# Other places in the DMA queues for a fused gated-mix kernel's first rows, bias rows, gate rows and rows for sums

## Chip, cores and metric

One Trainium2 chip, one core. The time is the device time of one execution in microseconds (us), the median of several runs. Lower is better. The core has five engines that run their own instruction queues: TensorE (PE, with its weight loads shown apart as PEld), VectorE (DVE), ScalarE (ACT), GpSimd (POOL) and SyncE (SP). Transfers between main memory and the core's memory (DMAs) are issued from the queues of SP, ACT and POOL.

## What is computed

```python
x: [2048, 512]; wqkv: [512, 1536]; w_phi: [32, 16, 16]; wo: [512, 512]
w1: [512, 1792]; w2: [1792, 512]; b1, b2, gate_w                      # all float32

g   = sigmoid((x * gate_w).sum(-1, keepdims=True))
# A: linear attention, 32 heads of 16
q, k, v = heads(x @ wqkv)
pq, pk  = q @ w_phi, k @ w_phi                       # per head
phi     = lambda p: concat(softmax(p), softmax(-p))  # 32 features per head
kv, z   = phi(pk).T @ v, phi(pk).sum(over rows)
a       = concat_heads(phi(pq) @ kv / (phi(pq) @ z + 1e-6)) @ wo
# B: dense layer with squared ReLU
b       = relu(x @ w1 + b1) ** 2 @ w2 + b2
out     = g * a + (1 - g) * b
```

## The kernel before

Every float32 matrix product is made of three matmuls in a faster float format: each operand is split into a high part (`hi`, a copy by ScalarE) and a low part (`lo`, a subtraction by VectorE), and `mm3` adds hi*hi, hi*lo and lo*hi. So each weight or x tile that is loaded costs one ScalarE and one VectorE instruction before TensorE can use it (`split`, L64 and L67).

The rows of x are cut into four blocks of 512 (`NB`), each of four chunks of 128 (`NC`). The spine is a list of 56 work units: two sweeps over the hidden layer (7 pieces of 128 hidden columns each), in each sweep the four blocks, in each block the 7 pieces. Unit t makes `up` for a later piece (`u`, then bias, ReLU and square on ScalarE) and `down` for its own (`d`). Everything else is hung into this spine by hand: `at(slot, f, ...)` puts a step at a slot, two slots to a unit, and `run(slot)` calls the steps as the spine is traced. The first sweep carries the key and value side of the attention: the fold of `w_phi` into the key weights, then eight pairs of row chunks (`pair_steps`), pair p at slot 14 + 4.5p. A pair multiplies its rows with the folded weights in seven block products; some of these use sums and differences of rows (`sums`, four additions on POOL) and of weights (`joint`). Three of the weight combinations don't fit in the core's memory: they are stored in main memory once (`wkeep`, L214) and reloaded for each pair into three slots (`again`, L624, issued from ACT's queue right behind the read of the product before). The second sweep carries the query side and the output.

The steps that matter here:

- `start` loads the first x tiles and the first weights, one behind the other on SP's queue (`fetch`, L513), while ten warm-up matmuls run; the weights of the first piece come in a quarter of their own (`first_w(0, 0, 1)`).
- `joint_start` loads the four pieces of `wv` (L176); `tiles_fold` makes the fold on TensorE (L184), and four transposes on VectorE (`turned`, L197) turn it.
- `rows_alike` loads `gate_w` (`gwb`) and `b2` (`b2b`), repeated over 128 partitions (L843). `b2b` is first read where a block's output rows are begun (L876).
- `gate_load` loads a chunk's rows for the gate (L264, L266), 256 KB each; `gate_chunk` multiplies and sums them on VectorE (L271); `gates` ends a block's gates.
- `x_load(b)` loads the four x tiles of a block (L87); block 2's go out on POOL's queue. `x_split` splits them.
- `sums_load(p)` loads the rows for a pair's sums (L596), `sums` adds them on POOL (L603 to L606) and splits them (`sh`, `sl`).
- At the end of a block in the first sweep its four chunks are stored to main memory from POOL's queue (`part`, L887).

Loads of x, of weights and of the rows for sums share four buffers (`in`), gate rows, output rows and some others share six (`row`). A load that has no free buffer waits in its queue, and what is queued behind it waits too.

The order on each queue is set by a scheduler when the kernel is built: it goes by the order in which the steps are traced and by when it thinks that buffers come free, so that a load whose buffer is free can be put ahead of an earlier one whose buffer isn't. `tc.issue_after(i)` pins instructions of the same engine behind `i` in the queue; it is an order, not a wait. `st[...]` holds the instructions that serve as such pins, among them `row` (the last of the first weight rows), `summed` (the last addition of a pair), `stored` (the last store on POOL's queue). `behind()` pins splits and gate work behind the latest split of a hidden piece.

```python
s = b * SL + 2.5 * c - 1 if b > 1 else 17.5 + c / 2 if b else 3.5 + 2 * c   # slot of chunk c's gate rows
at(s + (4.5 if b == 1 else 3), gate_chunk, b * NC + c)
s, late = ((4, 2), (19.5, 1), (22, 2.5), (36, 2))[b]                        # slot of x_load(b + 1)
at(s - 2 - (p > 0), sums_load, p)                                          # s: the pair's first slot
```

Of the kernel before, what the change touches and what calls it, by code (L numbers as in the profile page):

```python
# [8 lines left out]
F32 = mybir.dt.float32  # L9
# [7 lines left out]
P = 128  # L17
S, D, H, DH, F = 2048, 512, 32, 16, 1792
NK = D // P
# [16 lines left out]
def tile_gated_mix(ctx: ExitStack, tc: tile.TileContext, xT, xn, wqT, wkT, wphi, wv, wo, w1, b1, w2, b2, gw, out):  # L36
# [47 lines left out]

    def load(src, eng=nc.sync):
        t = stage.tile([P, 512], F32, tag="in", name="in")
        eng.dma_start(t, src)  # L87
        return t

    def row():  # L90
        return work.tile([P, D], F32, tag="row", name="row", bufs=6)
# [73 lines left out]
    def joint_start(loaded):  # L165
        wph, *t = loaded
        two = lambda a: a.rearrange("p (h c) -> p h c", h=2)
        st["W"], st["raw"] = {}, {}
        tmp = work.tile([P, 4 * D], F32, tag="phiT", name="tmp", bufs=1)
        st["tmp"] = tmp[:, :2 * D], tmp[:, 2 * D:]  # L170
        st["slots"] = [work.tile([P, 2 * D], F32R, tag=t, name=f"slot{t}", bufs=1) for t in ("o0", "o1", "ez")]
        for k in (0, 2, 1, 3):
            r = st["tmp"][k // 2] if k % 2 else work.tile([P, 2 * D], F32, tag="e", name=f"raw{k}", bufs=2)
            st["raw"][k] = r
            with tc.issue_after(st["row"].ins):
                nc.sync.dma_start(two(r)[:, :, 256:], two(wv[k * P:(k + 1) * P, :]))  # L176

    def tiles_fold(loaded):
        wph, *t = loaded
# [78 lines left out]


    def gate_load(n):  # L260
        st["xn", n] = row()
        if n // NC == 1:
            with tc.issue_after(st["summed"].ins):
                nc.gpsimd.dma_start(st["xn", n], xn[n])  # L264
        else:
            nc.sync.dma_start(st["xn", n], xn[n])  # L266

    def gate_chunk(n):
        t = st["xn", n]
# [229 lines left out]
    def start():  # L499
        fs, wide = range(FIRST), FIRST * P  # L500
        W = [ffn_tiles("w1", f) for f in fs]
        ps = [p.tile([P, SB], F32, tag="s", name="u") for p in (ps_e, ps_b, ps_f)]
        xs = st["x", 0] = []
        for f in fs:
            up_w[f] = [tuple(z[:, P * f:P * (f + 1)] for z in W[k]) for k in range(NK - 1)]
            up_w[f].append(tuple(z[:, wide:] for z in W[f]))
        raw = [(stage.tile([P, 512], F32, tag="in", name="in"), row()) for _ in range(NK)]
        last = act = None

        def fetch(dst, src):  # L510
            nonlocal last
            with tc.issue_after(last.ins) if last else nullcontext():
                last = nc.sync.dma_start(dst, src)  # L513

        def first_w(k, a, b):
            fetch(raw[k][1][:, a * P:b * P].rearrange("p (f c) -> p f c", f=b - a),
                  w1[a:b, :, k * P:(k + 1) * P].rearrange("f p c -> p f c"))

        def follow(i, eng, *a):
            with tc.issue_after(i.ins) if i else nullcontext():  # L520
                return eng(*a)

        ready = small.tile([P, 1], F32, tag="den", name="ready", bufs=2)
        act = nc.scalar.activation(ready, st["zeros"][:, :1], AF.Copy)
        for k in range(NK):
            if k == 0:
                first_w(k, 0, 1)
            fetch(raw[k][0], xT[0, :, k, :])
            first_w(k, 0 if k else 1, FIRST)
        dve = None  # L530
        for k in range(NK):
            u, t = raw[k]
            xh, xl = (xpool.tile([P, SB], F32R, tag=g, name=f"{g}0_{k}") for g in ("xh", "xl"))
            xs.append((xh, xl))
            if k == 0:
                w = [(t[:, a:b], *(z[:, a:b] for z in W[k])) for a, b in ((0, P), (P, wide))]
            elif k < NK - 1:
                w = [(t[:, :wide], *(z[:, :wide] for z in W[k]))]
            else:
                w = [(t[:, P * f:P * (f + 1)], *(z[:, wide:] for z in W[f])) for f in fs]  # L540
            if k < 2:
                dve = follow(dve, nc.vector.tensor_copy, xh, u)
            else:
                act = follow(act, nc.scalar.activation, xh, u, AF.Copy)
            for src, hi, lo in w:
                act = follow(act, nc.scalar.activation, hi, src, AF.Copy)
            lows = [(lo, src, hi.bitcast(F32), ALU.subtract) for src, hi, lo in w]
            lows.insert(k == 0, (xl, u, xh.bitcast(F32), ALU.subtract))
            for x in lows:
                dve = follow(dve, nc.vector.tensor_tensor, *x)  # L550
            terms = [(f, 0, xh) for f in fs] + [(f, 0, xl) for f in fs] + [(f, 1, xh) for f in fs]
            if k == 0:
                terms.insert(1, terms.pop(6))
            if k == NK - 1:
                terms.sort(key=lambda x: x[0])
            for n, (f, part_, x) in enumerate(terms):
                st["up"] = follow(st["up"], lambda: nc.tensor.matmul(
                    ps[f], up_w[f][k][part_], x, start=k == 0 and (part_, x) == (0, xh),
                    stop=k == NK - 1 and part_ == 1))
        fetch(b1c, b1)  # L560
        do_w1(FIRST)
        for f in fs:
            hid[f] = hidden(f, ps[f])
            if f == 0:
                st["act0"] = st["act"]
        for p in (ps_e, ps_b, ps_f):
            used(p)

    def x_load(b):
        if b == 2:  # L570
            with tc.issue_after(st["summed"].ins):
                st["xin", b] = [load(xT[b, :, k, :], nc.gpsimd) for k in range(NK)]
        else:
            st["xin", b] = [load(xT[b % NB, :, k, :]) for k in range(NK)]
        st["x", b] = []
# [15 lines left out]
    def sums_load(p):  # L591
        b, c = ROWS[p]
        rows = xT[b].rearrange("p k (h c r) -> p k h c r", h=2, c=2)[:, :, :, c, :]
        st["rows", p] = [stage.tile([P, 2, 2, P], F32, tag="in", name="in") for _ in range(2)]
        for i, t in enumerate(st["rows", p]):
            nc.sync.dma_start(t, rows[:, 2 * i:2 * i + 2])  # L596

    def sums(p):
        a, d = st["rows", p]
# [180 lines left out]
        at(14.5, joint_last, j)  # L780
    for b in range(NB):
        for c in range(NC):
            s = b * SL + 2.5 * c - 1 if b > 1 else 17.5 + c / 2 if b else 3.5 + 2 * c
            at(s, gate_load, b * NC + c)
            at(s + (4.5 if b == 1 else 3), gate_chunk, b * NC + c)
        if c == NC - 1:
            at(s + 4.5 if b == 1 else s + 3, gates, b)
        s, late = ((4, 2), (19.5, 1), (22, 2.5), (36, 2))[b]
        at(s, x_load, b + 1)
        for k in range(NK):  # L790
            at(s + late + k / 2, x_split, b + 1, k)
# [51 lines left out]
            nc.sync.dma_start(t, src.partition_broadcast(P))  # L843

    at(2, rows_alike, gwb, gw)
    at(9, rows_alike, b2b, b2)
    warm_up()
    start()
    with tc.issue_after(st["act0"].ins):
# [85 lines left out]
```

## Time and profile before

| | |
|---|---|
| median of 3 runs | 511.15 us (511.1 to 512.4) |
| profiled execution | 512.31 us, span 510.5 us from first to last instruction |
| TensorE busy | 502.9 us (99%) |
| VectorE busy | 407.1 us (80%) |
| ScalarE busy | 256.6 us (50%) |
| POOL busy | 91.4 us (18%) |
| granted TensorE clock | 1.00 |
| moved by DMA | 76.13 MB, 149 GB/s on average |

All times inside the trace are microseconds from the start of the span. A row of a timeline gives the start, the duration, the engine, the line of the kernel, the operation and `out<-in`; `x4` means four instructions taken together, and what stands in brackets is the time that the engine was idle before and what ended it. `SPq` and `ACTq` are the queues of these engines, and a DMA row shows the issue, not the transfer. In the chain, a DMA's time runs from issue to landing. TensorE's busy time counts overlapping matmuls once; consecutive full matmuls start 0.23 us apart in most of the span.

### The profile page before, as it was taken

The page shows a single profiled execution, that of the slowest core. Times are in us where ns is not written, and L with a number is a line of the kernel's source. Part 1 is how long each engine was busy: PE and PEld are TensorE (multiplying, and loading weights), DVE is VectorE, ACT ScalarE, POOL GpSimd, SP SyncE. Part 2 cuts the span into 40 slices and gives each one's busy share as a digit, 9 for nine tenths or more (in the row PEclk, how much of TensorE's full clock was granted, in tenths as well). Part 3 has the DMA queues.
Part 4 walks back from the last instruction along what each step waited for, and adds up shares of the span by engine and source line. Part 5 has one row for each costly group of instructions (what it writes and reads, how often), then busy time and mean ns, then how long its engine had stood idle before and what let it go on. Part 6 is the DMA issues. An engine that isn't in the chain of part 4 may idle for free.

```text
span 510.5 us, 9358 instructions
## 1 busy us (share of the span) xinstructions
PE 502.9 (99%) x3522; PEld 406.3 (80%) x3522; DVE 407.1 (80%) x675; ACT 256.6 (50%) x458; POOL 91.4 (18%) x105
## 2 busy tenths in 40 slices
PE   8999998999999999999999999999999999999997
PEld 5878776888888888888888878788787878788775
DVE  5559958798975979796987989897969797897724
ACT  4778753467344564463565654444455344333540
POOL 0000460203420033100012141211212120111200
PEclk9999999999999999999999999999999999999999
DMA  8768486756843559862276221325112221041112
GB/s 258 256 234 263 176 284 246 221 208 208 318 172 132 198 170 314 299 206 88 76 198 221 65 91 41 105 57 156 48 31 86 70 86 44 8 131 56 37 28 82
DMA packets 46757, 76.13 MB, mean 149 GB/s; under 512 B 6904, under 2 KB 24056, under 8 KB 46712
## 3 DMA queue, kind: packets, MB, share of 16 engines
q1 hardware_dynamic: 37304, 42.37, 27.2%
q10 hardware_dynamic: 6624, 23.73, 13.1%
q0 software_dynamic: 2784, 9.44, 5.2%
q8 instruction: 28, 0.46, 0.4%
q14 instruction: 17, 0.14, 0.1%
HBM read 57.68 MB, written 11.54 MB: 136 GB/s over the span
## 4 chain that ended last, share of the span: by engine, by line
PE 90%; DMA 5%; ACT 2%; DVE 1%; issue 1%; SPq 0%; DVEq 0%
PE u L77 9%; PE d L77 9%; PE d L78 9%; PE d L79 9%; PE u L78 9%; PE u L79 9%; PE pX L636 3%; PE q L77 3%; PE att L78 3%; PE att L77 3%; PE att L79 3%; PE q L79 3%; PE q L78 3%; PE pX L638 3%; PE pX L637 3%; DMA sloto<-wkeep 3%
## 5 line engine op out<-in xcount | busy, mean ns | idle before, releaser
L421 ACT ACTIVATE r<-u,b1c 128x512 f32<-128x512 f32 x56 | 38.5, 688 | 128.0 <-PE u L79 126.1
L77 PE MATMUL d<-w2h,hh 128*128 128x512 f32 x222 | 86.9, 392 | 0.0
L78 PE MATMUL d<-w2l,hh 128*128 128x512 f32 x222 | 86.5, 390 | 0.0
L79 PE MATMUL d<-w2h,hl 128*128 128x512 f32 x222 | 86.4, 389 | 0.0
L77 PE MATMUL u<-xh,w1h 128*128 128x512 f32 x212 | 83.8, 395 | 0.6 <-ACT w1h L64 0.6
L78 PE MATMUL u<-xl,w1h 128*128 128x512 f32 x212 | 82.6, 390 | 0.0
L79 PE MATMUL u<-xh,w1l 128*128 128x512 f32 x212 | 82.5, 389 | 0.0
L336 POOL TENSOR_TENSOR ez<-e,z 128x512 f32<-128x512 f32 x32 | 43.3, 1374 | 166.0 <-ACT e L308 166.0
L67 DVE TENSOR_TENSOR hl<-r,hh 128x512 fp32r<-128x512 f32 x56 | 38.6, 691 | 24.6 <-ACT hh L64 24.6
L77 PEld LDWEIGHTS u<-xh,w1h 128*128 128x128 f32 x212 | 39.8, 188 | 12.1 <-issue 2.9
L77 PEld LDWEIGHTS d<-w2h,hh 128*128 128x128 f32 x222 | 41.7, 188 | 9.2 <-issue 0.6
L78 PEld LDWEIGHTS d<-w2l,hh 128*128 128x128 f32 x222 | 41.7, 188 | 8.9 <-DVE w2l L67 0.4
L79 PEld LDWEIGHTS d<-w2h,hl 128*128 128x128 f32 x222 | 41.7, 188 | 8.7
L79 PEld LDWEIGHTS u<-xh,w1l 128*128 128x128 f32 x212 | 39.8, 188 | 8.4
L78 PEld LDWEIGHTS u<-xl,w1h 128*128 128x128 f32 x212 | 39.8, 188 | 7.9
L311 DVE TENSOR_REDUCE sm<-e 128x64 f32<-128x1024 f32 x27 | 32.8, 1214 | 10.5 <-ACT e L308 10.5
L308 ACT ACTIVATE e<-e 128x1024 f32<-128x1024 f32 x27 | 28.6, 1059 | 23.2 <-DVE e L306 23.1
L64 ACT ACTIVATE hh<-r 128x512 fp32r<-128x512 f32 x56 | 35.2, 628 | 1.0
L422 ACT ACTIVATE r<-r 128x512 f32<-128x512 f32 x56 | 34.9, 623 | 0.7
L675 ACT ACTIVATE tmp<-pX 128x512 f32<-128x512 f32 x24 | 14.4, 598 | 32.7 <-PE pX L638 30.9
L374 ACT ACTIVATE phiT<-tb 32x256 f32<-32x256 f32 x64 | 26.4, 412 | 5.0 <-DVE tb L359 3.9
L343 DVE TENSOR_REDUCE dz<-ez 128x64 f32<-128x1024 f32 x16 | 19.4, 1212 | 11.5 <-POOL ez L336 11.5
(179 smaller groups left out, 989.2 us busy)
## 6 DMA issues: line engine op xcount, KB each, us to landing
sloto<-wkeep ACTq DMA_DIRECT2D x30, 512.0 KB, 4.0
in<-in_xT SPq DMA_DIRECT2D x44, 256.0 KB, 3.9
slotez<-wkeep ACTq DMA_DIRECT2D x15, 512.0 KB, 4.1
phiT<-tb SPq DMA_DIRECT2D x192, 32.0 KB, 1.8
in<-in_w SPq DMA_DIRECT2D x23, 256.0 KB, 3.7
part<-row POOLq DMA_DIRECT2D x16, 256.0 KB, 5.3
row<-part SPq DMA_DIRECT2D x16, 256.0 KB, 2.8
out<-row SPq DMA_DIRECT2D x15, 256.0 KB, 2.2
```

The costliest lines, as they stand in the source:

```text
L64: i = nc.scalar.activation(hi, src, AF.Copy)
L67: st["lo"] = elo.tensor_tensor(lo, src, hi.bitcast(F32), ALU.subtract)
L77: nc.tensor.matmul(o, ah[:, sa], bh[:, sb], start=first, stop=False)
L78: nc.tensor.matmul(o, ah[:, sa], bl[:, sb], start=False, stop=False)
L79: return nc.tensor.matmul(o, al[:, sa], bh[:, sb], start=False, stop=last)
L308: nc.scalar.activation(ef, ef, AF.Exp)
L311: nc.vector.tensor_reduce(sm, e3, AX.X, ALU.add)
L336: nc.gpsimd.tensor_tensor(ez[:, hs, :], e3[:, hs, :], zbc[half], ALU.mult)
L343: nc.vector.tensor_reduce(dz, ez, AX.X, ALU.add)
L374: nc.scalar.activation(dst, src, AF.Copy)
L421: st["relu"] = nc.scalar.activation(r, ps, AF.Relu, bias=b1c[:, fc:fc + 1])
L422: nc.scalar.activation(r, r, AF.Square)
```

## The change

- In `start` the weights' first quarter is issued from ACT's queue, and the first x is the first load of SP's queue. The first activation is pinned behind that issue.
- The four `wv` loads lose their pin on `row`.
- `b2b` is loaded at slot 2 instead of 9.
- Block 0's gate rows: chunk 0 moves from slot 3.5 to 5.5, and its `gate_chunk` with it from 6.5 to 8.5; chunks 0 and 1 are pinned behind the last `wv` load, 2 and 3 behind the latest load made by `load` (`in`).
- Block 1's gate rows: chunks 0 and 1 stay at slots 17.5 and 18; 2 and 3 are loaded inside `x_load(2)`, behind the third and fourth x tile, all in one chain on POOL's queue.
- Gate rows of blocks 2 and 3 are pinned behind the latest rows for sums on SP's queue (`ahead`).
- Pair 4's rows for sums are loaded from POOL's queue, behind the latest store there.

```diff
--- before.py
+++ after.py
@@ -84,7 +84,7 @@
 
     def load(src, eng=nc.sync):
         t = stage.tile([P, 512], F32, tag="in", name="in")
-        eng.dma_start(t, src)
+        st["in"] = eng.dma_start(t, src)
         return t
 
     def row():
@@ -172,8 +172,7 @@
         for k in (0, 2, 1, 3):
             r = st["tmp"][k // 2] if k % 2 else work.tile([P, 2 * D], F32, tag="e", name=f"raw{k}", bufs=2)
             st["raw"][k] = r
-            with tc.issue_after(st["row"].ins):
-                nc.sync.dma_start(two(r)[:, :, 256:], two(wv[k * P:(k + 1) * P, :]))
+            st["wv"] = nc.sync.dma_start(two(r)[:, :, 256:], two(wv[k * P:(k + 1) * P, :]))
 
     def tiles_fold(loaded):
         wph, *t = loaded
@@ -258,12 +257,10 @@
 
 
     def gate_load(n):
+        eng, pin = ((nc.sync, "in" if n > 1 else "wv"), (nc.gpsimd, "summed"), (nc.sync, "ahead"), (nc.sync, "ahead"))[n // NC]
         st["xn", n] = row()
-        if n // NC == 1:
-            with tc.issue_after(st["summed"].ins):
-                nc.gpsimd.dma_start(st["xn", n], xn[n])
-        else:
-            nc.sync.dma_start(st["xn", n], xn[n])
+        with tc.issue_after(st[pin].ins):
+            st["xrow"] = eng.dma_start(st["xn", n], xn[n])
 
     def gate_chunk(n):
         t = st["xn", n]
@@ -513,20 +510,18 @@
                 last = nc.sync.dma_start(dst, src)
 
         def first_w(k, a, b):
-            fetch(raw[k][1][:, a * P:b * P].rearrange("p (f c) -> p f c", f=b - a),
-                  w1[a:b, :, k * P:(k + 1) * P].rearrange("f p c -> p f c"))
+            return (raw[k][1][:, a * P:b * P].rearrange("p (f c) -> p f c", f=b - a),
+                    w1[a:b, :, k * P:(k + 1) * P].rearrange("f p c -> p f c"))
 
         def follow(i, eng, *a):
             with tc.issue_after(i.ins) if i else nullcontext():
                 return eng(*a)
 
         ready = small.tile([P, 1], F32, tag="den", name="ready", bufs=2)
-        act = nc.scalar.activation(ready, st["zeros"][:, :1], AF.Copy)
+        act = follow(nc.scalar.dma_start(*first_w(0, 0, 1)), nc.scalar.activation, ready, st["zeros"][:, :1], AF.Copy)
         for k in range(NK):
-            if k == 0:
-                first_w(k, 0, 1)
             fetch(raw[k][0], xT[0, :, k, :])
-            first_w(k, 0 if k else 1, FIRST)
+            fetch(*first_w(k, 0 if k else 1, FIRST))
         dve = None
         for k in range(NK):
             u, t = raw[k]
@@ -568,8 +563,15 @@
 
     def x_load(b):
         if b == 2:
-            with tc.issue_after(st["summed"].ins):
-                st["xin", b] = [load(xT[b, :, k, :], nc.gpsimd) for k in range(NK)]
+            st["xin", b] = []
+            for k in range(NK):
+                with tc.issue_after(st["summed"].ins):
+                    t = stage.tile([P, 512], F32, tag="in", name="in")
+                    st["summed"] = nc.gpsimd.dma_start(t, xT[b, :, k, :])
+                    st["xin", b].append(t)
+                if k > 1:
+                    gate_load(NC + k)
+                    st["summed"] = st["xrow"]
         else:
             st["xin", b] = [load(xT[b % NB, :, k, :]) for k in range(NK)]
         st["x", b] = []
@@ -593,7 +595,11 @@
         rows = xT[b].rearrange("p k (h c r) -> p k h c r", h=2, c=2)[:, :, :, c, :]
         st["rows", p] = [stage.tile([P, 2, 2, P], F32, tag="in", name="in") for _ in range(2)]
         for i, t in enumerate(st["rows", p]):
-            nc.sync.dma_start(t, rows[:, 2 * i:2 * i + 2])
+            if p == 4:
+                with tc.issue_after(st["stored"].ins):
+                    st["stored"] = nc.gpsimd.dma_start(t, rows[:, 2 * i:2 * i + 2])
+            else:
+                st["ahead"] = nc.sync.dma_start(t, rows[:, 2 * i:2 * i + 2])
 
     def sums(p):
         a, d = st["rows", p]
@@ -780,8 +786,9 @@
         at(14.5, joint_last, j)
     for b in range(NB):
         for c in range(NC):
-            s = b * SL + 2.5 * c - 1 if b > 1 else 17.5 + c / 2 if b else 3.5 + 2 * c
-            at(s, gate_load, b * NC + c)
+            s = b * SL + 2.5 * c - 1 if b > 1 else 17.5 + c / 2 if b else max(5.5, 3.5 + 2 * c)
+            if b != 1 or c < 2:
+                at(s, gate_load, b * NC + c)
             at(s + (4.5 if b == 1 else 3), gate_chunk, b * NC + c)
         if c == NC - 1:
             at(s + 4.5 if b == 1 else s + 3, gates, b)
@@ -843,7 +850,7 @@
             nc.sync.dma_start(t, src.partition_broadcast(P))
 
     at(2, rows_alike, gwb, gw)
-    at(9, rows_alike, b2b, b2)
+    at(2, rows_alike, b2b, b2)
     warm_up()
     start()
     with tc.issue_after(st["act0"].ins):
```

## The prediction

> **What bounds the kernel now.** I read the page's head first, then who TensorE (PE) waits for, then the chain of work that ended last, and only then the timelines of the stretches that these name.
>
> ```profile
> span 510.5 us, 9358 instructions
> PE pX L636 <- DMA sloto<-wkeep: 1.9, 2, 1.7
> PE u L77 <- ACT w1h L64: 0.6, 1, 0.6
> PE u L557 <- DVE xh L521: 0.3, 1, 0.3
> ```
>
> The last three rows are PE's own waits (total, times, longest). PE waits for data 2.8 us in all, in three places, and the rest of the span is matmuls one behind the other, apart from the start-up and the last store. So no edit can win more than these waits and what it takes off the start. The chain puts them in time:
>
> ```profile
> 33.14 3.70 DMA in<-in_w
> ...
> 64.77 4.71 DMA sloto<-wkeep
> ...
> 70.59 8.41 DMA sloto<-wkeep
> 79.04 0.50 PE pX L636
> ```
>
> The 0.6 is a weight piece issued at 33.14, split by ScalarE (ACT) and needed by `u`. The 1.7 is the reload at 70.59: it takes 8.41 us where the one at 64.77 took 4.71, and PE stands until 79.04. The third is the first x tile.
>
> **The change, part by part.**
>
> **1. The start.** The first x goes ahead of the first weights' quarter on SP's queue, and the quarter goes out on ACT's.
>
> ```profile
> 0.74 0.39 SPq L513 DMA_DIRECT2D row<-in_w  x1
> 1.19 0.41 SPq L513 DMA_DIRECT2D in<-in_xT  x1
> 0.74 1.28 ACT L524 ACT_TABLE_LOAD   x1 [0.74 <-PEq L924]
> 2.71 0.31 ACT L521 ACTIVATE w1h<-row 128x128 fp32r<-128x128 f32 x1 [0.48 <-DMA row<-in_w]
> 5.33 0.43 DVE L521 CAST xh<-in 128x512 fp32r<-128x512 f32 x1 [4.20 <-DMA in<-in_xT]
> 1.19 4.45 PE L496 MATMUL warm<-zeros 128*128 128x512 bf16 x10 [1.19 <-DVE zeros L490]
> 5.91 0.77 PE L557 MATMUL u<-xh,w1h 128*128 128x512 f32 x1 [0.27 <-DVE xh L521]
> 6.47 0.60 PE L557 MATMUL u<-xh,w1l 128*128 128x512 f32 x1
> 6.90 0.63 PE L557 MATMUL u<-xh,w1h 128*128 128x512 f32 x2
> 7.36 0.85 PE L557 MATMUL u<-xl,w1h 128*128 128x512 f32 x3
> ```
>
> The x's issue moves from 1.19 to 0.74, so all that hangs on it moves up 0.45 us at most. ACT gets one issue ahead of its table load, about 0.4 us by SP's first row; the weights' split at 2.71 may come that much later and is still over 2 us ahead of the x at 5.33, which hides it. Ten warm-up matmuls take 4.45 us, 0.45 each; the third real one starts 0.43 behind the second, and from 6.90 on two take 0.46, so 0.23 each. The array is slow until about 6.7. If that is a matter of time, a start 0.45 sooner buys one more slow matmul and loses 0.20 of it: worth 0.25 us. If it is a matter of how many matmuls went before, the whole 0.45 stays. I take 0.25, since warm-ups and real matmuls were equally slow over 5 us; the ends are 0 (the tile lands no sooner) and 0.45.
>
> The Trainium skill's page "TensorE: Matmul & The Clock Gate", section "Part 1: The HAM clock gate (the "warmup" mystery)", says that the clock opens after a busy window of some 3.4 us that runs freely, a matter of time and not of the number of matmuls; it speaks against this part, and by it the start is worth 0.25, by a count 0.45. The slow spacing up to 6.7, 5.5 us behind the first warm-up, agrees with a gate, though the granted clock of this profile reads full speed throughout, and one switch in one run can't tell time from count.
>
> **2. Bias rows at slot 2, wv without its pin, first gate rows later.**
>
> ```profile
> 28.62 0.59 SPq L843 DMA_DIRECT2D b2b<-in_b  x1
> 29.25 1.70 SPq L266 DMA_DIRECT2D row<-in_xn  x3
> 27.26 2.51 PE L184 MATMUL fold<-row 32*32 32x128 f32 x128
> 29.43 0.68 DVE L271 SCALAR_TENSOR_TENSOR row<-row,gwb 128x512 f32<-128x512 f32 x1
> 30.04 2.50 DVE L197 STREAM_TRANSPOSE turned<-fold 128x512 f32<-128x512 f32 x4
> 35.89 0.69 DVE L67 TENSOR_TENSOR sloto<-raw,sloto 128x512 fp32r<-128x512 f32 x1 [2.17 <-ACT sloto L64]
> ```
>
> Just ahead of the late weight piece (33.14) SP issues b2b and three gate rows, 256 KB each and 1.05 MB together. b2b, the four wv pieces and the first two gate rows now go earlier, the last two gate rows behind the last weights of this stage. Gate chunk 0 (slot 6.5 to 8.5) leaves the place at 29.43, ahead of the transposes. These can then start when `fold` ends (27.26 + 2.51 = 29.77) and not at 30.04, 0.27 sooner, and with a start 0.25 sooner about 0.5. The piece at 33.14 waits for an x buffer that is freed behind the transposes, so it is issued 0.5 sooner as well and lands beside 1.05 MB less. PE's 0.6 goes: +0.6, with 0 the other end, should other transfers fill the gap.
>
> But this does not reach the end as it stands:
>
> ```profile
> 35.00:54.00 19.00, 18.39 (x82) 14.88 (x81) 17.41 (x31) 16.66 (x31) 2.84 (x5) 1.00 0.62 205
> 57.35 0.60 ACT L675 ACTIVATE tmp<-pX 128x512 f32<-128x512 f32 x1 [0.93 <-DMA wkeep<-spare]
> 58.27 0.69 ACT L421 ACTIVATE r<-u,b1c 128x512 f32<-128x512 f32 x1 [0.32 <-PE u L79]
> 58.85 1.14 ACT L64 ACTIVATE sh<-in 128x512 fp32r<-128x512 f32 x2
> ```
>
> The columns of the window's row are PE, PEld, DVE, ACT, POOL. From 35.89 to the end of this stage VectorE (DVE) never rests for long: 17.41 of 19 us, with most of the rest ahead of 35.89. Chunk 0's 0.61 us (29.43 to 30.04) now falls into it and takes back the 0.5 that the transposes won. What PE needs next, `sh` at 58.85, hangs on that chain: ACT came free at 57.95 (57.35 + 0.60) of a read that the store of `spare` held back, which VectorE's split feeds, and then idled only 0.32 for PE. So PE can be at most 0.32 sooner here, though parts 1 and 2 give 0.25 + 0.6 = 0.85. I take 0.2 for both together: under 0.32, as VectorE comes about 0.1 later. The ends are 0 and, should the scheduler put chunk 0 where VectorE has room, 0.85.
>
> **3. The reload at 70.59.** Two of block 1's four gate rows move behind the third and fourth x tile on POOL's queue, and the first row of block 2 behind rows for sums on SP's.
>
> ```profile
> 69.28 2.16 POOL L264 DMA_DIRECT2D row<-in_xn  x4
> 71.43 1.06 POOL L87 DMA_DIRECT2D in<-in_xT  x2
> 81.80 0.54 POOL L87 DMA_DIRECT2D in<-in_xT  x1 [9.30 <-DVE sl L67]
> 71.39 0.34 SPq L266 DMA_DIRECT2D row<-in_xn  x1
> q0 software_dynamic: 475, 1.56, 56.3%
> q10 hardware_dynamic: 302, 1.10, 33.5%
> q1 hardware_dynamic: 127, 0.24, 7.9%
> ```
>
> The last three rows are the queues from 70.6 to 79.0: POOL (q0) moved 1.56 MB, ACT (q10) with the reloads 1.10, SP (q1) 0.24, together 2.90 MB in 8.4 us or 345 GB/s. The third x tile waits for a buffer until 81.80, and what is queued behind it waits too, so two rows (0.52 MB) leave this window, and SP's row (0.24). That leaves 1.10 + 1.04 = 2.14 MB, 6.2 us at 345 GB/s: the reload lands at 76.8. Should ACT keep only its share while POOL has work, POOL's 1.04 MB last until 76.2 at 186 GB/s, ACT has moved 0.73 by then and the other 0.37 take 1.1 us alone: 77.3. PE stood 1.7 us before 79.04, so it needs the tile at 77.3. Either way the wait goes: 1.6, with 0 as the other end. Cover: the two late rows are read by chunks two or more slots behind, and the x tiles keep their places; the two that are free go 1.08 us sooner. The 0.2 that is left of the 1.9 belongs to the reload at 64.77, ahead of all this: it stays.
>
> **4. Rows for sums of pair 4 on POOL, later gate rows pinned.** PE's list of waits has nothing behind 79, so nothing is to be won here.
>
> ```profile
> 130.37 0.75 POOL L603 TENSOR_TENSOR in<-in 128x256 f32<-128x256 f32 x1
> 155.10 0.39 PE L636 MATMUL pX<-slotez,sh 128*128 128x512 f32 x1
> in<-in_xT POOLq DMA_DIRECT2D x4, 256.0 KB, 7.2
> ```
>
> The adds of pair 4 run at 130.37 now, right behind POOL's stores; the two loads come between. At 7.2 us from issue to landing the adds begin near 139, and PE reads their splits at 155.10: about 16 us cover two loads, the adds (under 5 us) and the splits, so I cost this at 0. Without that cover it would be some 8 us of waiting. What is queued behind on POOL is the adds of the next pair, needed later still.
>
> **Sum.** 0.2 + 1.6 = 1.8 us. The profiled execution took 512.31 us (its span 510.5 and 1.8 around it), which gives 510.5; it lay 1.16 above the runs' median of 511.15, from which the same sum gives 509.35. Predicted 509.3 us. Anything under 0.3%, 1.5 us, can't be told from no change on this kernel.
>
> **The rivals.**
>
> Everything reaches the end: chunk 0 finds room on VectorE, so 0.85 + 1.6 plus the 0.2 at 64.77 gives 2.65 and 508.5 us. For it: the 2.17 us of idle VectorE at 35.89. Against: chunk 0 is pinned behind that stage's splits.
>
> The reload is not relieved: the third x tile's buffer comes free early, so that the x tiles fill the window in place of the gate rows. Then 0.2 is all, 510.95 us. Against it stand the 9.30 us which that tile waited; it would have to be issued before about 75.
>
> Slower: wv's four pieces (1.05 MB) lose the pin that held them behind the first weight rows, their tiles are free from the beginning, and they get into SP's queue ahead of the first x.
>
> ```profile
> 0.00:4.20 4.20, 3.01 (x8) 1.09 (x9) 0.27 (x1) 1.79 (x3) 1.16 (x10) 1.00 0.44 74
> 0.00:7.30 7.30, 5.84 (x14) 2.55 (x15) 2.20 (x7) 2.41 (x5) 1.16 (x10) 1.00 0.71 189
> ```
>
> The last column is GB/s: by 4.2 us 0.31 MB were moved, the first quarter and the first x, whose cast came at 5.33, 1.1 later; 1.38 MB are moved by 7.3. With wv ahead the cast comes at 8.4, 3.1 us late. Less the 1.6 of part 3 that is 512.65 us. It decides from a delay of 1.6 us on, and is told from no change at about 3.1. Against it: SP's queue issues without a gap from 0.74 on, and the first loads come first in the program.
>
> **How the numbers follow.** The forecast 0.55 (own range 508.8 to 510.2), everything reaches the end 0.15, no relief 0.16, wv ahead 0.09, and 0.05 for a wait that a new order puts elsewhere. Faster by over 0.3% (under 509.6): 0.15 and seven tenths of the forecast's 0.55, 0.53. Slower by over 0.3% (over 512.7): the upper part of wv ahead and most of the unnamed, with some of it out of the forecast's own reordering, 0.12. The rest, 0.35, is no change. The range takes in the rival with all gains and the one without relief: 508.0 to 511.9; it leaves out wv ahead and the unnamed.
>
> **What would show it.** Right: the first `u` matmul at 5.4 to 5.7 and the third still slow; PE's wait for `w1h` gone; DVE's L271 no longer ahead of the transposes; `sh` near 58.6; on POOL two gate rows, two x tiles, then a gap of some 10 us; the reload near 70 landing in about 6 us and PE's wait for it under 0.3. Wrong: wv among SP's first issues; a PE wait for `sh` or `sl` near 59; a new PE wait for `wkeep` after 80, where the two moved rows now land; a wait for `sh` near 155.

## The result, and the profile after

The changed kernel takes 508.37 us (median of six executions, 507.6 to 508.76) against 511.32 us before (six, 510.52 to 512.4): 2.95 us less, a ratio of 0.9936 with a 95% interval of 0.9921 to 0.9952. The forecast was 509.3 us, with the range 508.0 to 511.9. The total is inside it, but in good part by luck: the runs below show that both terms of its sum, 0.2 for parts 1 and 2 and 1.6 for part 3, had been put at the wrong parts.

The head of the page of the changed kernel, and who PE waits for (total, times, longest):

```profile
span 506.6 us, 9362 instructions
...
PE warm L493 <- DVE zeros L487: 1.2, 1, 1.2
PE pX L644 <- DVE sl L67: 0.5, 1, 0.5
```

The waits for `w1h`, for the reload and for the first x are gone. One new wait has come, 0.5 us for `sl`. Row by row, the start-up (timeline of the changed kernel; where DVE, ACT or PE idled before a row, the bracket says how long and for what):

```profile
0.74 0.41 ACTq L521 DMA_DIRECT2D row<-in_w  x1
0.74 0.39 SPq L510 DMA_DIRECT2D in<-in_xT  x1
...
4.88 0.43 DVE L518 CAST xh<-in 128x512 fp32r<-128x512 f32 x1 [3.75 <-DMA in<-in_xT]
...
5.06 0.63 ACT L518 ACTIVATE w1h<-row 128x128 fp32r<-128x128 f32 x2 [2.39 <-DMA row<-in_w]
...
5.45 0.47 PE L552 MATMUL u<-xh,w1h 128*128 128x512 f32 x1
...
6.08 0.62 PE L552 MATMUL u<-xh,w1h 128*128 128x512 f32 x2
```

x is cast at 4.88 instead of 5.33 and the first `u` comes at 5.45 instead of 5.91, 0.46 sooner. The weights' split, though, went from 2.71 to 5.06.

The stretch of the fold, and the first pair:

```profile
26.71 1.91 PE L183 MATMUL fold<-row 32*32 32x128 f32 x128
...
28.61 2.51 DVE L196 STREAM_TRANSPOSE turned<-fold 128x512 f32<-128x512 f32 x4 [0.41 <-PE fold L183]
...
31.72 5.16 SPq L87 DMA_DIRECT2D in<-in_w  x3
...
34.63 0.69 DVE L67 TENSOR_TENSOR sloto<-raw,sloto 128x512 fp32r<-128x512 f32 x1 [2.34 <-ACT sloto L64]
...
36.21 0.50 PE L77 MATMUL u<-xh,w1h 128*128 128x512 f32 x1
...
58.67 0.17 DVE L276 TENSOR_SCALAR rest<-gate 128x4 f32<-128x4 f32 x1
58.78 0.69 DVE L67 TENSOR_TENSOR sl<-in,sh 128x512 fp32r<-128x512 f32 x1
...
59.53 0.50 PE L644 MATMUL pX<-slotez,sl 128*128 128x512 f32 x1 [0.52 <-DVE sl L67]
```

The `u` that comes at 36.21 came behind a wait in the kernel before, and so did the product that now comes at 68.31 (further below):

```profile
38.19 0.50 PE L77 MATMUL u<-xh,w1h 128*128 128x512 f32 x1 [0.61 <-ACT w1h L64]
...
69.61 0.47 PE L636 MATMUL pX<-sloto,sh 128*128 128x512 f32 x1 [0.20 <-DMA sloto<-wkeep]
```

So the `u` is 1.98 us sooner. Of these, 1.15 are there at the end of the fold: it ends at 28.62 and not at 29.77, because it starts 0.55 sooner and takes 1.91 us instead of 2.51. At 59.53 part of it is lost: block 0's gates stand ahead of `sl` on VectorE.

The reloads and POOL's rows, in the same kernel, and the two windows of ten microseconds, the changed kernel's ahead of that of before (columns PE, PEld, DVE, ACT, POOL, granted clock, DMA share, GB/s):

```profile
60.84 0.33 ACTq L630 DMA_DIRECT2D sloto<-wkeep  x1
...
68.31 0.39 PE L642 MATMUL pX<-sloto,sh 128*128 128x512 f32 x1
...
69.11 1.10 POOL L263 DMA_DIRECT2D row<-in_xn  x2
...
69.19 0.33 ACTq L630 DMA_DIRECT2D sloto<-wkeep  x1
...
75.80 0.39 PE L642 MATMUL pX<-sloto,xh 128*128 128x512 f32 x1
...
503.34 0.48 DVE L441 SCALAR_TENSOR_TENSOR row<-last,rest,row 128x256 f32<-128x256 f32 x1 [0.23 <-PE last L79]
```

```profile
69.00:79.00 10.00, 10.00 (x46) 8.29 (x45) 7.71 (x13) 5.55 (x11) 2.27 (x5) 1.00 0.76 273
```

```profile
69.00:79.00 10.00, 8.17 (x35) 6.11 (x33) 7.18 (x12) 4.60 (x8) 3.50 (x7) 1.00 0.96 346
...
506.92 0.48 DVE L444 SCALAR_TENSOR_TENSOR row<-last,rest,row 128x256 f32<-128x256 f32 x1 [0.23 <-PE last L79]
```

PE now works through the window in which it had stood 1.83 of 10 us. The lead of the changed kernel over the profiled one of before is 0.46 us at the first `u`, 1.98 at 36.21, 1.30 at 68.31, 3.24 at 75.80 (79.04 less 75.80) and 3.58 at the last row (506.92 less 503.34). So over half of it comes from the stretch between 68 and 79, as forecast, but look at the first row of the reloads: of the two that used to be issued together at 64.77, one is issued at 60.84, ahead of the read at 64. No line of the change touches the reloads. The scheduler has put them in another order on ACT's queue.

### The profile page after: what moved, and what is told of

Read it like the earlier page. It is cut to its first block, busy times and chain, and to the rows that moved or that the text cites. A ratio compares the mean times of both kernels' runs of the same rounds, so it can differ in the third digit from the quotient of the medians.

```text
span 506.6 us, 9362 instructions
## 1 busy us (share of the span) xinstructions
PE 501.5 (99%) x3522; PEld 405.7 (80%) x3522; DVE 405.5 (80%) x675; ACT 256.4 (51%) x458; POOL 92.4 (18%) x107
## 4 chain that ended last, share of the span: by engine, by line
PE 94%; DVE 4%; DMA 1%; issue 1%; ACT 0%; DVEq 0%; ACTq 0%
PE d L77 9%; PE d L78 9%; PE d L79 9%; PE u L77 9%; PE u L79 9%; PE u L78 9%; PE pX L642 3%; PE q L77 3%; PE att L77 3%; PE att L79 3%; PE att L78 3%; PE q L79 3%; PE q L78 3%; PE pX L644 3%; PE pX L643 3%; PE pY L644 2%
```

## The experiments

All times are in us; each kernel of a series was run beside the kernel before. A ratio is not the quotient of the two medians beside it, and it leaves out the two single executions named in the table and two of the kernel before (1375.27 and 1295.67). PE's waits come from one profiled execution each, without the wait of the warm-up.

| kernel | median (range) | before, median | ratio (95% interval) | PE's waits over 0.25 |
|---|---|---|---|---|
| before, again | 511.68 (508.82 to 514.42) | 511.07 | 0.9997 (0.9972 to 1.0021) | x 0.3 |
| part 1 alone | 511.4 (508.91 to 513.63) | 511.07 | 0.9991 (0.9965 to 1.0017) | reload 1.7, `w1h` 0.6 |
| part 2 alone | 509.63 (507.98 to 511.65) | 511.07 | 0.9955 (0.9933 to 0.9977) | `sh` 1.0 |
| part 3 alone | 512.06 (508.87 to 512.52, one of 2870.06) | 511.07 | 0.9984 (0.9960 to 1.0009) | `w1h` 1.7, reload 1.6 |
| after, again | 508.53 (507.55 to 509.02, one of 556.97) | 511.70 | 0.9952 (0.9934 to 0.9970) | `w1h` at the start 0.4, reload 0.3, `sh` 0.3 |
| parts 1 and 2 | 509.25 (508.09 to 509.9) | 511.70 | 0.9961 (0.9944 to 0.9978) | `sh` 0.3 |
| before, reload early | 510.15 (508.93 to 511.4) | 511.70 | 0.9981 (0.9959 to 1.0003) | x 0.8 |
| after, reload late | 509.05 (508.11 to 510.04) | 511.70 | 0.9960 (0.9943 to 0.9977) | `sh` 0.6 |
| part 2 alone, reload late | 510.3 (509.04 to 512.16) | 511.75 | 0.9967 (0.9944 to 0.9989) | reload 0.8 |
| bias rows alone | 511.08 (508.3 to 513.32) | 511.75 | 0.9978 (0.9952 to 1.0004) | none |
| parts 1 and 3, pins of part 4 | 511.18 (510.54 to 511.84) | 511.75 | 0.9984 (0.9962 to 1.0007) | reload 1.6 |
| after, gates later | 508.69 (508.13 to 510.27) | 511.75 | 0.9935 (0.9913 to 0.9956) | `r` 0.4 |

### The kernel before, once more

No edit.

> The kernel before, unchanged, as a second profile and as the measure of what two equal programs differ by. Both theories: the time within 0.2% of the other runs of it. What the profile tells apart: the first profile of it lay about 1 us above its median, with two places where TensorE lost time that no data explains: the first real matmuls 0.56 and 0.43 us apart, and 2.51 us for the fold's 128 small matmuls against 1.91 after the change. If these belong to that one execution, this profile shows a fold of about 1.9 us and other spacings at the start; if they belong to the program (the first gate chunk and the bias rows near the fold, a later start), it shows them again.

Its twelve executions spread over 5.6 us. The profiled one took 508.82 us, the least of them. PE's waits, the timeline, and the loading of the reloaded weights (PEld) for the product that had waited until 79.04:

```profile
PE u L557 <- DVE xh L521: 0.3, 1, 0.3
...
68.88 2.15 POOL L264 DMA_DIRECT2D row<-in_xn  x4
...
68.96 0.33 ACTq L624 DMA_DIRECT2D sloto<-wkeep  x1
...
75.68 0.19 PEld L636 LDWEIGHTS pX<-sloto,xh 128*128 128x128 f32 x1 [0.38 <-DMA sloto<-wkeep]
```

The waits for `w1h` and for the reload, 2.5 us together, aren't there. So they belong to some executions of the program and not to all: the profile that the prediction was read from, at 512.31, showed an execution with both. In this one the reload is issued 0.08 us behind POOL's four gate rows, in the other 1.31 behind (70.59 less 69.28). It still takes 6.7 us, and PE comes to it just as it lands. Against this execution the changed kernel has no lead in the stretch of the reloads: its two products stand at 68.31 and 75.80, these at 68.09 and 75.69. Over its three series the kernel before has medians of 511.07 to 511.75 and best times of 508.78 to 509.28; the changed one 508.37 and 508.53, best times of 507.6 and 507.55. So the best times are 1.2 to 1.7 us apart (of 35 executions against six and twelve), the medians about 3. This suggests that the change takes away a common mishap more than it shortens an undisturbed execution.

### Part 1 alone

```diff
...
-        act = nc.scalar.activation(ready, st["zeros"][:, :1], AF.Copy)
+        act = follow(nc.scalar.dma_start(*first_w(0, 0, 1)), nc.scalar.activation, ready, st["zeros"][:, :1], AF.Copy)
         for k in range(NK):
-            if k == 0:
-                first_w(k, 0, 1)
             fetch(raw[k][0], xT[0, :, k, :])
...
```

> The kernel before with the start alone changed: the first x first on SP's queue, the weights' first quarter on ACT's. Theory of the prediction: the start is worth 0.25 us and VectorE's full stretch before the first sums lets at most 0.32 through, so 510.9 to 511.3 where before has 511.3. Rival, the start reaches the end in full: 0.45 to 0.6 us, near 510.8, with every later mark (fold, reload) sooner by the same. Rival, nothing arrives, because the wait for the first-layer weights near 38 us or for the reload near 79 us grows by what the start won: no change, and the waits longer by 0.4.

The first `u` comes at 5.36, so the 0.45 us are there, and nothing of it can be told in the time. Both waits are as before. A start sooner by less than half a microsecond is below what twelve executions with this spread can show.

### Part 2 alone

```diff
...
-            with tc.issue_after(st["row"].ins):
-                nc.sync.dma_start(two(r)[:, :, 256:], two(wv[k * P:(k + 1) * P, :]))
+            st["wv"] = nc.sync.dma_start(two(r)[:, :, 256:], two(wv[k * P:(k + 1) * P, :]))
...
+        elif n // NC == 0:
+            with tc.issue_after(st["in" if n > 1 else "wv"].ins):
+                nc.sync.dma_start(st["xn", n], xn[n])
...
-            s = b * SL + 2.5 * c - 1 if b > 1 else 17.5 + c / 2 if b else 3.5 + 2 * c
+            s = b * SL + 2.5 * c - 1 if b > 1 else 17.5 + c / 2 if b else max(5.5, 3.5 + 2 * c)
...
-    at(9, rows_alike, b2b, b2)
+    at(2, rows_alike, b2b, b2)
```

> The kernel before with only this changed: bias rows at slot 2, the pin of wv taken off, block 0's gate rows later and gate chunk 0 at slot 8.5. Theory of the prediction: the wait of 0.6 for the first-layer weights near 38 us goes, but VectorE's full stretch takes back all but some 0.2, so 511.1. Rival from the trace after the change: VectorE starts that stretch over 1 us sooner since the transposes no longer stand behind the gate chunk and the fold is quicker, and 0.5 to 1 us arrives: 510.3 to 510.8. In both the reload near 79 us still makes TensorE wait 1.5 us or more.

This part alone is faster, by 1.4 us in the medians, with an interval that ends below 1. In its profile the reload wait is gone although all four gate rows of block 1 still go out at 69.93, in the stretch where the prediction saw the cause in them. The reload of the odd slot is issued at 61.67, so it is this part that reorders ACT's queue. In this profile PE waits 1.0 us anew for `sh`.

### Part 3 alone

```diff
...
-                st["xin", b] = [load(xT[b, :, k, :], nc.gpsimd) for k in range(NK)]
+            for k in range(NK):
+                with tc.issue_after(st["summed"].ins):
+                    t = stage.tile([P, 512], F32, tag="in", name="in")
+                    st["summed"] = nc.gpsimd.dma_start(t, xT[b, :, k, :])
+                    st["xin", b].append(t)
+                if k > 1:
+                    gate_load(NC + k)
+                    st["summed"] = st["xrow"]
...
```

(and the pins of the later gate rows).

> The kernel before with only this changed: two of block 1's gate rows behind the third and fourth x tile on POOL's queue, and the gate rows of blocks 2 and 3 pinned behind the rows for sums on SP's. All theories: the reload that is issued near 70.6 lands in 6 to 7 us in place of 8.4 and TensorE's wait for it of 1.7 us goes to under 0.3; 1.4 to 1.7 us, 509.6 to 509.9. What would tell against it: the reload lands as late as before, since the two x tiles and the other reloads fill the time; then no change.

PE's waits and the timeline of part 3 alone:

```profile
PE u L77 <- ACT w1h L64: 1.7, 1, 1.7
PE pX L644 <- DMA sloto<-wkeep: 1.6, 2, 1.4
...
69.51 1.11 POOL L267 DMA_DIRECT2D row<-in_xn  x2
70.61 1.07 POOL L576 DMA_DIRECT2D in<-in_xT  x2
...
70.99 0.33 ACTq L632 DMA_DIRECT2D sloto<-wkeep  x1
...
79.11 0.50 PE L644 MATMUL pX<-sloto,xh 128*128 128x512 f32 x1 [1.36 <-DMA sloto<-wkeep]
```

The rows are moved as the prediction said: two on POOL instead of four, and 310 GB/s in the window 69 to 79 instead of 346. The reload still takes 8.07 us (70.99 to 79.06) and PE still waits. The step of the prediction on which 1.6 of its 1.8 us rested, that fewer bytes in the window bring the reload in after 6.2 us, doesn't hold by itself. An x tile now goes out at 70.61, ahead of the reload, where the third gate row had gone.

### Parts 1 and 3 with the pins of part 4

The changed kernel without part 2 and without pair 4's loads on POOL's queue.

> Parts 1 and 3 with the pins of part 4, without part 2: b2b and block 0's gate rows as before. The prediction gave part 3 the larger part, 1.6 us: then 0.996 to 0.997. Theory that part 2 carries the change: 0.998 to 1.000, with a reload near 70 of 7 to 8 us and a wait of over 0.5 us for it, or a wait for w1h near 37 of over 0.5 us, in the trace.

```profile
PE pX L642 <- DMA sloto<-wkeep: 1.6, 2, 1.3
...
68.84 0.47 PE L642 MATMUL pX<-sloto,sh 128*128 128x512 f32 x1 [0.28 <-DMA sloto<-wkeep]
...
68.48 1.10 POOL L267 DMA_DIRECT2D row<-in_xn  x2
...
69.80 0.33 ACTq L630 DMA_DIRECT2D sloto<-wkeep  x1
...
77.86 0.50 PE L642 MATMUL pX<-sloto,xh 128*128 128x512 f32 x1 [1.30 <-DMA sloto<-wkeep]
```

The same again: two rows fewer, and the wait stays. All twelve executions (510.54 to 511.84) lie above all but one of the changed kernel's twelve in its second series (507.55 to 509.02, and a single 556.97), beside medians of before of 511.75 and 511.70. Without part 2 (and pair 4's loads) the change is worth nothing that can be told from zero here.

### Parts 1 and 2

> The kernel before with the start and the part of bias rows, wv and block 0's gate rows, but with block 1's four gate rows together as before. Theory of the prediction (bytes): the reload near 70 us lands in 7 to 8.5 us beside 1 MB of gate rows, TensorE waits 1 to 1.7 us for it, 0.997 to 1.000 of before. Theory formed from the traces (order): what frees that reload is not the two rows that are gone but that in this order ACT's queue issues the reload before it near 61 us instead of 65, so that the two no longer stand one behind the other; then no wait here either, and the time within 0.15% of the changed kernel's.

PE's waits:

```profile
PE pX L636 <- ACT sh L64: 0.3, 1, 0.3
PE att L79 <- DVE o L67: 0.2, 1, 0.2
```

No wait for a reload, with all four gate rows at 69.36. The median is 2.45 us under before, the changed kernel's in the same series 3.17; the two intervals overlap widely. So parts 3 and 4 add some 0.7 us in the medians, and perhaps nothing.

### The order of the reloads by itself: four kernels

The reload of the odd slot early in the kernel before, with no other change:

```diff
-            with tc.issue_after(read.ins):
+            with tc.issue_after(read.ins), tc.high_priority(offset=AHEAD) if i == 1 else nullcontext():
                 again(p, i, 1)
```

> The kernel before with one thing changed that is no part of the change: the reload of the third product's first half is queued right behind the read of the first product on ACT (near 57.5 us) instead of near 65. Theory of order: the waits for reloads near 69 and 79 us go (1.9 us in the first profile), the wait of 0.6 for weights near 38 stays, and the time is 0.996 to 0.9975 of before. Theory of bytes: the wait near 79 stays at 1 us or more, since block 1's gate rows are all there, and no more than 0.2 to 0.3 us is won.

The changed kernel with the first pair's two reloads together near 64, as before:

```diff
             with tc.issue_after(read.ins):
-                again(p, i, 1)
+                if p or i not in (1, 6):
+                    again(p, i, 1)
+                if (p, i) == (0, 5):
+                    with again(p, 1, 1):
+                        again(p, 6, 1)
```

> The changed kernel with the first pair's two reloads put together again on ACT's queue near 65 us, as they stood before; the two gate rows stay behind the x tiles. Theory of order: a wait for reloads of 1 us or more near 68 and 76 us comes back and takes back half of the gain, 0.996 to 0.998 of before. Theory of bytes: the reload still lands in time since 0.8 MB less moves beside it; a wait of 0.2 to 0.3 near 68 at most, and the time stays within 0.1% of the changed kernel's.

The same edit on part 2 alone:

> Part 2 alone (bias rows at slot 2, wv without its pin, first gate rows later), with ACT's queue as in the kernel before: the pair's two reloads stand together again behind the third read (near 64 to 65) instead of one at 61. Theory 'the earlier reload carries the gain of part 2': the ratio returns to 0.999 or above, and the trace shows a PE wait of 0.5 to 1.9 us for a reload near 70 to 79. Rival 'the weight piece near 33 is what counts, the reload's place is by the way': 0.995 to 0.997, as part 2 alone had, and no wait for a reload over 0.5 us.

And the bias rows alone, which leave the reloads where they were:

> Only the bias rows moved, from slot 9 to slot 2; gate rows, wv, start and reloads as before (the gate rows are still issued just ahead of the weight piece near 33). Theory 'the four loads of 1.05 MB ahead of that piece delay it': 0.26 MB less beside it, so a little, 0.997 to 1.000. Rival 'the reload's place carries part 2': reloads stand as before, so 0.999 to 1.001, with waits for a reload as in the kernel before.

PE's waits and the timeline of part 2 alone with the late reload:

```profile
PE pX L638 <- DMA sloto<-wkeep: 0.8, 1, 0.8
...
64.32 0.81 ACTq L626 DMA_DIRECT2D sloto<-wkeep  x2
...
68.87 2.16 POOL L263 DMA_DIRECT2D row<-in_xn  x4
...
69.71 0.33 ACTq L626 DMA_DIRECT2D sloto<-wkeep  x1
...
76.90 0.50 PE L638 MATMUL pX<-sloto,xh 128*128 128x512 f32 x1 [0.84 <-DMA sloto<-wkeep]
```

With the reload early the kernel before has no wait near 78, with the reload late part 2 alone has 0.8 us of it again. In the changed kernel, which has fewer rows there as well, late reloads bring nothing back. One profile of each proves little, since the kernel before has the wait in one of its two profiles. Over all fourteen, none of the six with an early reload has a wait near 78, and five of the eight with late reloads have one.

In the times the order alone is not proven: 0.9981 with an interval up to 1.0003 for the early reload, and part 2 has much the same gain to before with either order (1.44 and 1.45 us in the medians, 0.9955 and 0.9967). The time with late reloads is the one expected by the rival, by which the weight piece counts and the reload's place does not; the wait of 0.8 is the one expected by the theory of the order. So most of part 2's gain doesn't hang on the order. One profile of each shows what may have kept the early order from gaining more: 0.8 us at the reload with the one, 1.0 us at `sh` with the other. The bias rows alone (0.9978, up to 1.0004) can't be told from no change; whether `wv`'s pin or block 0's gate rows carry part 2 was not tried.

What goes with the wait in most profiles is how far the reload near 70 comes behind POOL's gate rows, and how many of POOL's loads (gate rows and x tiles, 256 KB each) are issued from 68 us on ahead of it:

| reloads | kernel | POOL's rows | reload | behind | loads ahead | reload takes | PE's wait near 78 |
|---|---|---|---|---|---|---|---|
| late | part 3 alone | 69.51 | 70.99 | 1.48 | 3 | 8.07 | 1.36 |
| late | part 1 alone | 68.38 | 69.75 | 1.37 | 3 | 8.24 | 1.49 |
| late | parts 1 and 3 | 68.48 | 69.80 | 1.32 | 3 | 8.02 | 1.30 |
| late | before | 69.28 | 70.59 | 1.31 | 3 | 8.41 | 1.66 |
| late | bias rows alone | 68.17 | 69.30 | 1.13 | 3 | not recorded | none |
| late | part 2, reload late | 68.87 | 69.71 | 0.84 | 2 | 7.14 | 0.84 |
| late | after, reload late | 68.44 | 69.11 | 0.67 | 2 | 5.8 | none |
| late | before, again | 68.88 | 68.96 | 0.08 | 1 | 6.7 | none |
| early | before, reload early | 68.81 | 69.54 | 0.73 | 2 | not recorded | none |
| early | after, twice | | | 0.08 each | 1 | 3.2, 3.9 | none |
| early | part 2; parts 1 and 2 | | | 0.08 each | 1 | not recorded | none |
| early | after, gates later | 70.78 | 68.92 | 1.86 ahead | 0 | 3.4 | none |

With three loads ahead the reload takes 8.0 to 8.4 us wherever its landing is recorded, with two 5.8 and 7.1, with none 3.4. With one it takes 3.2 and 3.9 in the changed kernel but 6.7 in the second profile of the kernel before, so the count isn't all of it. It fits that moving two rows did nothing in part 3 alone: an x tile took the third row's place ahead of the reload. In the bias rows alone the third load goes out just ahead of the reload, and PE doesn't wait.

Why the reload comes late against POOL is in part an argument. With late reloads the one at 64 lands as PE comes to it: PE stood for it 0.2 to 0.3 us at 69.61 before, and at 70.02, 68.79 and 68.84 in the first three rows. The next reload hangs on that product, so it slips by as much; the rest of the microsecond is that POOL's rows, which hang on additions, went out sooner against PE. In the profiles with early reloads PE passes there without a stop. No edit changed the number of loads ahead of the reload and nothing else, so it is not shown that this makes the landing slow; why it takes 8 us stays open.

### The gates later

To remove the changed kernel's new wait, 0.5 us for `sl`, block 0's gates are put behind the first split of the sums.

```diff
-        with behind():
+        with behind(), nullcontext() if b else tc.issue_after(st["sums0"].ins), nullcontext() if b else tc.high_priority(offset=AHEAD):
...
-            at(s + 4.5 if b == 1 else s + 3, gates, b)
+            if b:
+                at(s + 4.5 if b == 1 else s + 3, gates, b)
...
+        if p == 0:
+            at(13.5, gates, 0)
```

> The changed kernel with block 0's three gate instructions (1.1 us of VectorE) put behind the first split of the sums, so that the first sl no longer stands behind them; the scheduler then also queues the reload of (3,0) ahead of that of the odd slot. If the 0.5 us that PE waits for sl near 59 reaches the end: 0.4 to 0.5 us less than the changed kernel, so a ratio of 0.993 to 0.9945 to the kernel before. If the next read takes it back: as the changed kernel, 0.994 to 0.996.

PE's waits:

```profile
PE u L77 <- ACT r L418: 0.4, 1, 0.4
PE pX L642 <- DMA sloto<-wkeep: 0.2, 1, 0.2
```

The wait for `sl` is gone and ACT holds PE up instead, 0.4 us at 58.06. The median, 508.69, is that of the changed kernel (508.37 and 508.53). No kernel here beats it.

The changed kernel beside these:

> The changed kernel itself, for a second profile and for a ratio beside the other three. Both theories: 0.992 to 0.996 of before; no wait for the reload near 76 us and none for the first-layer weights near 36; a wait of about 0.5 us for sl near 59.

It repeats its result, 0.9952 with an interval of 0.9934 to 0.9970, and PE has four waits of 0.2 to 0.4 us behind the warm-up and none above. The wait for `sl` isn't among them, so it too belongs to some executions.

## Why the prediction was right or wrong, step by step

**The start: gain right, cover wrong.** The first `u` came 0.46 us sooner. But the weights' quarter on ACT's queue was to be "still over 2 us ahead of the x", hidden. It wasn't: its split moved by 2.35 us, not by 0.4, and now ends together with the cast of x. In the second profile of the changed kernel it decides. Its chain of waits and its timeline:

```profile
0.74 4.28 DMA row<-in_w
...
1.19 3.77 PE L493 MATMUL warm<-zeros 128*128 128x512 bf16 x10 [1.19 <-DVE zeros L487]
...
5.41 0.49 PE L552 MATMUL u<-xh,w1h 128*128 128x512 f32 x1 [0.44 <-ACT w1h L518]
```

64 KB, issued at 0.74 beside the x, took 4.28 us; on SP's queue ahead of it, it had landed by 2.71. The step priced the issue and not the company in which the transfer travels. The Trainium skill's page "DMA: Bandwidth & Descriptors", section "Queues, rings and completion order", says that a transfer's completion is reported only behind every earlier write of the same DMA engine, across its queues; a quarter that reports just as the x does agrees with it, though no run here separates that from plain sharing.

"The third still slow" was wrong for the profiled execution: its third `u` came 0.32 behind the second (6.08 less 5.76; 0.43 before), and the two of its row, 0.62 together, are 0.23 apart. The change is not the reason, as the last section shows.

**Parts 1 and 2, 0.2 us: too small, and this is the term that carried the change.** Together they measured 2.45 us in the medians (0.9961, some 2.0 us). Over the fourteen profiles PE waits over half a microsecond for `w1h` or for the reload near 78 in four of the seven kernels without part 2, and in one of the seven with it (0.84, the reload put late). Three things were missed. The fold: the transposes were to start 0.5 us sooner and start 1.43 sooner (28.61 for 30.04), 0.6 of it because the fold of the profiled execution was itself slow, 2.51 us; in the second profile of the kernel before it takes 1.91 as well. VectorE's full stretch was to take everything back beyond 0.32 us at `sh`; but the first `sloto` split moved up 1.26 us (35.89 to 34.63), and with it the whole chain, so the product that reads `sh` came 1.48 us sooner (59.53 to 58.05). And the scheduler: dropping a pin and moving loads on SP's queue changed the order on ACT's, which the prediction took as fixed.

**Part 3, 1.6 us: the place and the size right, the reason wrong; here the sum was right by luck.** The wait at 79 went, but part 3 alone (1.6 us of wait left) and parts 1 and 3 (1.6) keep it. The step that failed is the sum of bytes: two rows and SP's row fewer in the window were to bring the reload in after 6.2 us, at 76.8, or at 77.3. With the two rows moved it took 8.07 and 8.02 us; an x tile had taken a row's place ahead of it. "The 0.2 that is left of the 1.9 belongs to the reload at 64.77, ahead of all this: it stays" failed too. That small stop is gone with one reload issued at 60.84, and the reload behind it then came with POOL's rows, not after them.

**Part 4, nothing: nothing speaks against it, though it was not run by itself.** The loads for pair 4 on POOL, and the additions behind them:

```profile
126.97 1.51 POOL L600 DMA_DIRECT2D in<-in_xT  x2
...
133.84 0.81 POOL L609 TENSOR_TENSOR in<-in 128x256 f32<-128x256 f32 x1 [5.36 <-DMA in<-in_xT]
```

The additions begin at 133.84, sooner than the 139 given, and PE's list has no wait behind them.

**The wrong signs listed.** wv did not go ahead of x; it is issued at 13.98. The wait for `sl` near 59 came, 0.52 us, and cost nothing that its removal could win back. The rival nearest to the measured time was "everything reaches the end", 508.5; its reason, chunk 0 finding room on VectorE, is at most a part: chunk 0 did move out of the way, to 39.65, and the 0.2 and the 1.6 of its 2.65 went, in the profiles above, with part 2 and not with part 3.

## What to carry to other kernels

A wait in one profile may belong to some executions alone: profile the unchanged kernel a second time before a sum is made of its waits. A small stop ahead of a large one is worth following: if the later transfer is issued behind the stopped product, the small stop delays it as well, and what other queues issue meanwhile gets ahead of it. And where a scheduler orders all queues, read the changed order on every queue, not on the edited one.

## What the runs showed of the hardware

The spacing of the first matmuls is not set by the kernel. With the first warm-up at 1.19 in each, the ten warm-ups took 3.77 us in the changed kernel's second profile and 4.45 in that of parts 1 and 2, where three more matmuls were slow:

```profile
1.19 4.45 PE L498 MATMUL warm<-zeros 128*128 128x512 bf16 x10 [1.19 <-DVE zeros L492]
...
6.72 0.81 PE L557 MATMUL u<-xh,w1h 128*128 128x512 f32 x2
...
7.37 0.85 PE L557 MATMUL u<-xl,w1h 128*128 128x512 f32 x3
```

In that kernel the array is slow until about 7.2 (0.81 for two, 0.85 for three), in the other only until some time before 5, as its ten warm-ups, 0.68 us shorter together, can't all have been slow. So the array opens neither a fixed time nor a fixed number of matmuls behind the first warm-up; the opening moves by more than two microseconds between these executions. The Trainium skill's page "TensorE: Matmul & The Clock Gate", section "Part 1: The HAM clock gate (the "warmup" mystery)", speaks of a window of time that runs freely; an opening that moves agrees with it, though the granted clock of these profiles reads full speed throughout. The 0.25 us that the prediction gave to the start, worked out from one opening at 6.7, is an estimate for that execution alone.

The same reload of 512 KB near 70 took 8.41 us before, 8.24, 8.07 and 8.02 in the three other profiles where it came 1.3 us or more behind rows on another queue, and 3.2 in the changed kernel, 0.08 behind them. Being close behind was not enough for that: in the second profile of the kernel before it took 6.7, also 0.08 behind.
